# Gated linear attention into a GELU feed-forward on one core: the first three units recast as six chunks with head halves on the partition halves

## The chip, the cores and the metric

The kernel runs on one core of one Trainium2 chip. The metric is device time in microseconds of one execution, given as the median of several runs. The engines are TensorE (PE in the views, with PEld for its weight loads), VectorE (DVE), ScalarE (ACT), GpSimd (POOL) and SyncE (SP, which here only issues transfers). Each takes its own instructions in the order in which the program lists them.

## The reference

Attention with a per-channel decay (a recurrence over 768 positions, 4 batches, 8 heads of 48 channels), and on its output a feed-forward network with exact GELU:

```python
f = 1.0 / (1.0 + np.exp(-f_logit))
for t in range(S):
    state = f[:, :, t, :, None] * state + np.einsum('bhd,bhe->bhde', k[:, :, t], v[:, :, t])
    y[:, :, t] = np.einsum('bhd,bhde->bhe', q[:, :, t], state)
x = y.transpose(0, 2, 1, 3).reshape(B * S, H * D)      # 3072 x 384
h = x @ w_in                                           # 384 x 2048
g = 0.5 * h * (1.0 + erf(h / sqrt(2)))
out = g @ w_out                                        # 2048 x 384
```

## The kernel before

The 3072 rows are 24 chunks of 128 positions, six to a batch. Two chunks make a unit; there are 12 units. Inside a chunk the recurrence is written as masked matrix products; between chunks a state of 48 x 48 per head is carried.

For each unit the steps are these. `decays` takes `fl` (the logits) through exp and ln on ACT (L494, L497), sums the logarithms along the positions on PE with a triangular matrix (L521, or L526/L527 with `trip` for paired units; L515 and L523 give the chunk's total), and makes `rg` and `gt`, the exponentials of minus and plus the sums (L543, L549). DVE multiplies k and q by them (L576) into `sc`; `vb` is v in bf16 (L583). `turn` transposes `sc` on PE (L611) and copies the result to `kq` (L617), or from unit 4 on uses a DMA transpose (L599). PE makes the scores (L722, paired L784), DVE masks them (L631), PE multiplies them by v (L758, paired L826) and adds the part from the carried state (L699, paired L705). The state product is L745 (paired L806); `carry` updates the state: `rr` on DVE (L655), `tn` on POOL (L657), and two copies into the diagonal blocks of `sb` (L662), whose other blocks stay zero. `outputs` copies y to `yb` (L675), transposes it (L691) and copies it to `xT` (L694).

Units 0 to 4 are paired (`PAIRS`): partition p of a tile holds positions 2p and 2p+1 of a stretch of 256, so that a load moves runs of 384 bytes rather than 192. The 64 upper partitions are then the second chunk of the unit. The output rows are put back in order by the gelu, which writes `gT` with a permuted pattern.

`ffn_group` takes one unit's 256 rows: eight F1 steps (L875, six matmuls each) fill a PSUM bank, gelu (L885) writes `gT`, and per chunk four F2 steps (L896, four matmuls each, one for each piece `wout0` to `wout3`) sum into another bank. The result goes through `osb` (L901) to DRAM (L906). Four PSUM banks (`s_fh`) are shared by F1, F2 and, for early units, sums and transposes; the other four by the rest of the attention.

Transfers are in a list, `LOADS`. SP issues the inputs (L449 paired, L457 for the rest), POOL the weights (L461 `win`, in pieces of 1024, 512 and 512 columns; L464 `wout`). Before the first piece of `win` stand f, k, v, q of units 0 and 1; unit 2's come after it, then the rest of `win` and `wout`, then unit 3. A transfer that follows one from the other queue waits for an earlier one there to land (`gate`).

The order on each engine comes from a planner, `Plan.run`, which places the operations one after another by priority. Here the priorities are formulas plus random offsets from `SEEDS`. Where the plan leaves PE idle in the first 30 us, matmuls on a zero tile `junk` (L947) are put in. ACT needs a table load (L953) at each change between exp/ln and gelu.

Of the kernel before, what the change touches and what calls it, by code (L numbers as in the profile page):

```python
# [2 lines left out]

# [9 lines left out]
ALU = mybir.AluOpType  # L13

LAT = {"PE": 0.25, "ACT": 0.16, "DVE": 0.14, "POOL": 0.12, "DMA": 1.0}
TABLE = 1.28

# [2 lines left out]
SHARED = 0.5  # L22

TURN = 0.1

SPREAD, SEED = (1.0, 97)

SEEDS = [1643, 41, 3215, 1275, 2533, 2502, 823, 887, 1264, 763, 2447, 3095]

NUDGE = {}  # L30
XA = 0.0

EAGER = 0.0

# [50 lines left out]
class Plan:  # L85

    def __init__(self):
        self.ops, self.w, self.r = [], {}, {}  # L90

# [24 lines left out]
    def run(self):  # L116
        free = dict.fromkeys(list(LAT), 0.7)
        free["DMA"] = 1.8
        rng = random.Random(SEED)
        own = [random.Random(x) for x in SEEDS]  # L120
        for o in self.ops:
            if o.prio > -5:
                k = min(max(int(o.prio % 1000) // 20, 0), len(SEEDS) - 1)
                o.prio += rng.uniform(-SPREAD, SPREAD)
                if SEEDS[k]:
                    w = (0.5, 1.0, 3.0, 8.0)[SEEDS[k] % 4]
                    o.prio += own[k].uniform(-w, w)
            o.prio += NUDGE.get(o.name, 0.0) + (XA if o.table == "exp" and o.prio > 40 else 0.0)
        act, switched, mode = None, 0.0, 0
        port = {"DVE": (0.0, 0.0), "POOL": (0.0, 0.0)}  # L130
        for o in self.ops:
            o.outs = []
        for o in self.ops:
            o.left = len(o.deps)
            for d in o.deps:
                d.outs.append(o)
        ready = [o for o in self.ops if not o.left]
        placed = []
        while ready:
            best = None  # L140
            for o in ready:
                t = free[o.eng]
                for d in o.deps:
                    v = d.end if d.eng == o.eng and (o.eng != "DMA" or d is o.chain) else d.vis + o.lag
                    t = v if v > t else t
                ok, taken = True, {}
                for b in o.bufs:
                    if b.slot is None:
                        v, k = b.slots.free(), taken.get(id(b.slots), 0)
                        if len(v) <= k:  # L150
                            ok = False
                            break
                        t = max(t, v[k][0])
                        taken[id(b.slots)] = k + 1
                if not ok:
                    continue
                x = t
                if o.table and act and o.table != act:
                    x = max(t, min(t + 2 * TABLE, max([d.vis for d in o.deps] + [switched]) + PATIENCE))
                pr = o.prio + (HOLD if o.held and act == "gelu" else 0.0)  # L160
                key = (int((x - (EAGER if o.eng == "PE" and o.prio < 900 else 0.0)) * 20 + 0.999), pr, o.seq)
                if best is None or key < best[0]:
                    best = (key, t, o)
            if best is None:
                raise RuntimeError("no operation can be placed: %s" % [o.name for o in ready[:20]])
            _, t, o = best
            d = o.dur
            if o.eng == "PE" and o.mode != mode:
                mode = o.mode
                d += TURN  # L170
            if o.port:
                other = port["POOL" if o.eng == "DVE" else "DVE"]
                d += SHARED * max(0.0, min(other[1], t + d) - max(other[0], t))
            if o.table and o.table != act:
                act, switched = o.table, t
                d += TABLE
            o.start, o.end = t, t + d
            o.vis = o.end + o.lat
            free[o.eng] = o.end
            for b in o.bufs:  # L180
                if b.slot is None:
                    b.slot = b.slots.free()[0][1]
                    b.slots.who[b.slot] = b
                b.slots.memo = None
            ready.remove(o)
            placed.append(o)
            if o.port:
                port[o.eng] = (t, o.end)
            for n in o.outs:
                n.left -= 1  # L190
                if not n.left:
                    ready.append(n)
        if len(placed) != len(self.ops):
            raise RuntimeError("operations that wait for each other")
        placed.sort(key=lambda o: (o.start, o.seq))
        self.placed = placed
        return placed

SIZES = [2, 2, 2, 2, 2, 2, 2, 2, 2, 2, 2, 2]
PAIRS = [0, 1, 2, 3, 4]
WIN = [1024, 512, 512]
EG = [0, 1]
ET = [0, 1]
EX = [0]
EA = [0]
SPLIT = []  # L220
HVC = [1]
HKQ = [0, 2, 6]
HYB = [1, 5]
HX = [4]
GKP, GQP = ([2], [3])
GAM = []
ODVE = [0, 1, 2, 4, 6, 7, 8, 9, 10, 11, 12, 13, 14, 16, 17, 18, 19, 20, 21, 22, 23]
XDMA = [5, 6, 7, 8, 9, 10, 11]
KDMA = [4, 5, 6, 7, 8, 9, 10, 11]
AJ = [2, 3, 4, 5, 6, 7, 8, 10, 11]  # L230
NGT = 4
GLD = []
G1D = [2, 3, 4]
YJ = [2, 3, 4]
ROWS = [16, 17, 18, 19]
AMX = []
WARM = 30.0
LOADS = ['f0', 'k0', 'v0', 'q0', 'f1', 'v1', 'k1', 'q1', 'i0', 'k2', 'f2', 'v2', 'q2', 'i1', 'i2', 'i3', 'o0', 'o1', 'o3', 'o2', 'f3', 'k3', 'q3', 'u4', 'v3']
LOADS += [f"u{n}" for n in range(12) if f"u{n}" not in LOADS and f"c{2 * n}" not in LOADS and f"f{n}" not in LOADS]


@with_exitstack
def kernel(
# [59 lines left out]
    s_sb = slots(3, [C, P2, 2 * D], BF16, "sb")  # L303
    s_yb = slots(3, [C, 2, HD], BF16, "yb")
    s_os = slots(4, [C, d_model], F32, "osb")
    s_xT = {s: slots({1: 4, 2: 4}.get(s, 2), [C, s, KO, C], BF16, f"xT{s}") for s in set(SIZES)}
    s_gT = {s: slots({1: 4, 2: NGT}.get(s, 2), [C, FO, s * C], BF16, f"gT{s}") for s in set(SIZES)}
    banks = [pp.tile([C, 512], F32, name=f"ps{i}") for i in range(8)]
    nf, na, _ = BANKS
    s_fh, s_m = Slots(nf, banks[:nf]), Slots(8 - nf - na, banks[nf + na:])  # L310
# [9 lines left out]
    P.add("POOL", 0.5, lambda: make_identity(nc, ident), wr=["ident"], prio=-90)  # L320
    P.add("POOL", 0.5, lambda: tri(mask, 1.0), wr=["mask"], prio=-80)
    P.add("POOL", 0.1, lambda: nc.gpsimd.memset(negcol, -1.0), wr=["negcol"], prio=-79)

    def pair_sums():
# [32 lines left out]
    z_gl = [f"glz{i}" for i in range(6)]  # L359
    z_lf = [f"lfz{i}" for i in range(3)]  # L360
    z_sc = [f"scz{i}" for i in range(NQ)]
    z_sb = [f"sbz{i}" for i in range(3)]

    G = [dict(xT=s_xT[SIZES[g]].new(), gT=s_gT[SIZES[g]].new()) for g in range(NG)]
# [2 lines left out]
        for j in range(SIZES[g]):  # L367
            grp[first[g] + j] = (g, j)
    X = [{} for _ in range(NCH)]
    U = [dict(fl=s_fl.new(), lf=s_lf.new(), pair=u in PAIRS, **{nm: s_in[nm].new() for nm in s_in}) for u in range(NU)]  # L370

    def half(u, b, j):

# [2 lines left out]
        return b.t().rearrange("p (j h d) -> p j h d", j=2, d=D)[:, j]  # L376

    order, pools = [], []  # L380

    def load(eng, issue, wr, bufs, dur, name):
        i = len(order)
        gate = None
        if i and order[i - 1][0] != eng:
            back = 4 if eng == "pool" else 2
            for j in range(i - back, -1, -1):
                if order[j][0] != eng:
                    gate = order[j][1]
                    break  # L390

        def fn(o):
            ins = issue()
# [30 lines left out]
    def srcp(a, u):  # L424
        b, c = divmod(2 * u, nC)
        return a[b, :, c * C:(c + 2) * C, :].rearrange("h (p j) d -> p h (j d)", j=2)

    win_src = moe_w_in.rearrange("(kk p) f -> p kk f", p=C)
    wo_src = moe_w_out.rearrange("(r p j) m -> r p j m", r=4, j=4)
    for what in LOADS:  # L430
        m = int(what[1:])
        if what[0] in "ucfkqv":
            js = (0, 1)
            if what[0] == "c":
                js, m = (m % 2,), m // 2
# [31 lines left out]
    def decays(u):  # L467
# [37 lines left out]
        for j, n in enumerate(ns):  # L505
# [68 lines left out]
            for w, nm, a, b, off in ((0, "kp", "kt", rg, 0), (1, "qp", "qt", gt, 1)):  # L574
# [8 lines left out]
            P.add("ACT" if hv else "POOL", 0.40 if hv else 0.47, lambda y=y, j=j, hv=hv: (nc.scalar.copy if hv else nc.gpsimd.tensor_copy)(  # L583
                y["vb"].t().rearrange("p (h d) -> p h d", h=H), half(u, x["vt"], j)),
                rd=[("vt", n)], wr=[("vb", n)], bufs=[y["vb"], x["vt"]], prio=pr, name=f"VC{n}")

    St = {}

# [177 lines left out]
    def attn_pair(u):  # L766
# [86 lines left out]
        for cc, n in enumerate(ns):  # L853
            outputs(n, yps[cc])

    def ffn_group(g):
        s, t = SIZES[g], G[g]
        xT, gT = t["xT"], t["gT"]
# [9 lines left out]
        for u in range(FO // pk):  # L868
# [10 lines left out]
                  wr=[("h", g, u)], bufs=[xT, hps, gT], prio=pr, opens=hps, name=f"F1.{g}.{u}")  # L879
            def gelu(u=u, hps=hps):  # L880
                to, fr = gT.t()[:, u * pk:(u + 1) * pk, :].rearrange("p a b -> p (a b)"), hps.t()
                if U[ns[0] // 2]["pair"]:
                    to = to.rearrange("p (n t j) -> p n j t", j=2, t=64)
                    fr = fr.rearrange("p (n j t) -> p n j t", j=2, t=64)
                nc.scalar.activation(to, fr, AF.Gelu)  # L885
            P.add("ACT", 0.60 if U[ns[0] // 2]["pair"] else 0.50, gelu, rd=[("h", g, u)], wr=[("gT", g, u)], bufs=[hps, gT], table="gelu", prio=pr - 1000,
                  name=f"GE{g}.{u}")
        for s_ in range(s):
            n = first[g] + s_
# [3 lines left out]
            for r in range(4):  # L893
                def f2(s_=s_, r=r, op=op):
# [6 lines left out]
            P.add("DVE" if od else "ACT", 0.475 if od else 0.40, lambda op=op, osb=osb, od=od: copier(not od)(osb.t(), op.t()[:, 0:d_model]),  # L901
                  rd=[("o", n)], wr=[("os", n)], bufs=[op, osb], prio=pr - 1000, name=f"O{n}")
            def store(n=n, osb=osb):
                w = C // 2 if n in ROWS else C
                for r in range(0, C, w):
                    nc.sync.dma_start(out=out[n * C + r:n * C + r + w, :], in_=osb.t()[r:r + w, :])  # L906
# [18 lines left out]
                name=f"st{n}")  # L925

    g = 0
    for u in range(NU):
        decays(u)
        (attn_pair if U[u]["pair"] else attn_nat)(u)  # L930
        while g < NG and first[g] + SIZES[g] <= 2 * u + 2:
            ffn_group(g)
            g += 1
# [53 lines left out]
```

## Time and profile before

| | |
|---|---|
| median of 3 runs | 182.42 us (182.16 to 182.50) |
| span of the profiled execution | 181.1 us |
| granted PE clock | 1.000 |
| PE, DVE, ACT, POOL busy | 171.7, 96.3, 125.2, 53.6 us |
| DMA | 32.61 MB, mean 180 GB/s |
| gelus on ACT (L885) | 96, 57.5 us, 671 ns each |
| table loads on ACT (L318, L953) | 16, 1283 ns each |
| first F1 matmul, last matmul's end | 20.67, 178.1 us |

The span runs from the first to the last instruction of the execution that was profiled; that execution has no separate time of its own in the results, so the 1.3 us between the span and the median of the runs are what lies around it. Matmuls overlap, so the mean duration of one (273 ns for L875) is not the distance between two (109 ns); for costs the distance is used. Bytes are counted as they arrive: weights are read as float32 and arrive as bf16.

### The profile page before, as it was taken

What the parts mean: (1) busy time and instruction counts of PE and PEld (TensorE: products, weight loads), DVE (VectorE), ACT (ScalarE), POOL (GpSimd) and SP (SyncE); (2) the same over time, 40 slices, a digit from 0 to 9 for tenths busy, and PEclk for the clock granted to TensorE, in tenths of its full rate; (3) what the DMA queues carried; (4) which work ended last, traced back from release to release, by engine and by line L of the source; (5) the groups of instructions that cost most, each with busy time, mean ns of one, the idle gap of its engine ahead of it and who ended that gap; (6) DMA issues with size and microseconds to landing.
All of it is one profiled execution on the core that took longest, in us unless ns stands there. A gap on an engine that the chain in (4) does not pass through costs nothing.

```text
span 181.1 us, 4916 instructions
## 1 busy us (share of the span) xinstructions
PE 171.7 (95%) x1990; PEld 132.3 (73%) x1990; DVE 96.3 (53%) x194; ACT 125.2 (69%) x212; POOL 53.6 (30%) x116
## 2 busy tenths in 40 slices
PE   7788889999999999988999999999999999999993
PEld 2356669966787688785779689976697986886972
DVE  5289750058898564244896692527691625362110
ACT  2775198963899189999967759777585578560720
POOL 7657870003043641140176113112435110300000
PEclk9999999999999999999999999999999999999999
DMA  6999999949997898999999999999999872814102
GB/s 148 261 261 226 268 170 203 200 115 267 278 266 142 186 197 170 249 227 171 216 179 213 215 175 207 195 187 189 185 245 181 181 162 47 166 37 91 43 0 87
DMA packets 106998, 32.61 MB, mean 180 GB/s; under 512 B 102113, under 2 KB 106081, under 8 KB 106977
## 3 DMA queue, kind: packets, MB, share of 16 engines
q1 hardware_dynamic: 105056, 29.07, 79.7%
q0 software_dynamic: 1776, 3.15, 9.8%
q8 instruction: 15, 0.25, 0.6%
q10 hardware_dynamic: 144, 0.10, 0.2%
q14 instruction: 7, 0.05, 0.1%
HBM read 25.17 MB, written 4.72 MB: 165 GB/s over the span
## 4 chain that ended last, share of the span: by engine, by line
PE 64%; ACT 15%; DMA 15%; SPq 3%; issue 1%; DVE 0%; DVEq 0%
PE ps L875 26%; PE ps L896 25%; ACT gT L885 7%; DMA fl<-in_f_logit_dram 7%; DMA win<-in_moe_w_in_dram 5%; ACT L953 4%; SPq L449 3%; DMA kq<-sc 2%; PE ps L722 2%; PE ps L758 2%; PE ps L917 1%; ACT gt L549 1%; PE ps L521 1%; PE ps L699 1%; PE ps L745 1%
## 5 line engine op out<-in xcount | busy, mean ns | idle before, releaser
L885 ACT ACTIVATE gT<-ps 128x512 bf16<-128x512 f32 x96 | 57.5, 671 | 24.6 <-PE ps L875 23.0
L875 PE MATMUL ps<-xT,win 128*128 128x256 bf16 x576 | 68.7, 273 | 1.3 <-ACT gT L885 0.9
L896 PE MATMUL ps<-wout,gT 128*128 128x384 bf16 x368 | 66.0, 326 | 0.0
L875 PEld LDWEIGHTS <-win 128*128 128x128 bf16 x576 | 61.6, 114 | 3.9 <-issue 1.2
L896 PEld LDWEIGHTS <-gT 128*128 128x128 bf16 x368 | 34.2, 98 | 19.5
L583 POOL CAST vb<-vt 128x384 bf16<-128x384 f32 x22 | 12.6, 584 | 52.5 <-DMA vt<-in_v_dram 52.4
L631 DVE TENSOR_TENSOR am<-ps,mask 128x512 bf16<-128x512 f32 x28 | 17.6, 684 | 15.1 <-PE ps L722 15.1
L901 DVE COPY osb<-ps 128x384 f32<-128x384 f32 x20 | 11.1, 556 | 25.9 <-PE ps L896 18.2
L657 POOL TENSOR_TENSOR tn<-rr,gl 128x384 f32<-128x384 f32 x16 | 14.0, 872 | 35.2 <-DVE rr L655 34.6
L576 DVE TENSOR_TENSOR sc<-qt,gt 128x384 bf16<-128x384 f32 x23 | 14.0, 616 | 13.7 <-ACT gt L549 13.7
L576 DVE TENSOR_TENSOR sc<-kt,rg 128x384 bf16<-128x384 f32 x23 | 13.5, 597 | 11.3 <-ACT rg L543 11.3
L953 ACT ACT_TABLE_LOAD x15 | 19.2, 1283 | 0.3
L662 POOL CAST sb<-tn 48x192 bf16<-48x192 f32 x40 | 14.8, 371 | 11.6 <-DVE tn L651 6.6
L494 ACT ACTIVATE fl<-fl 128x768 f32<-128x768 f32 x12 | 10.1, 842 | 10.5 <-DMA fl<-in_f_logit_dram 10.5
L675 DVE CAST yb<-ps 128x384 bf16<-128x384 f32 x22 | 11.9, 555 | 7.4 <-PE ps L758 3.7
L631 DVE TENSOR_TENSOR am<-ps,maskp 128x512 bf16<-128x512 f32 x20 | 12.5, 684 | 2.2 <-PE ps L784 1.4
L543 ACT ACTIVATE rg<-ps 128x384 f32<-128x384 f32 x21 | 10.3, 503 | 4.4 <-PE ps L523 2.8
L549 ACT ACTIVATE gt<-ps 128x384 f32<-128x384 f32 x21 | 10.2, 503 | 3.9 <-PE ps L523 3.3
L947 PE MATMUL ps<-junk 128*128 128x512 bf16 (+3 forms) x36 | 10.4, 423 | 2.1 <-POOL junk L939 1.3
L655 DVE TENSOR_TENSOR rr<-ps,tn 128x384 f32<-128x384 f32 x16 | 8.9, 553 | 3.5 <-POOL tn L657 1.8
L497 ACT ACTIVATE lf<-fl 128x768 bf16<-128x768 f32 x12 | 10.1, 843 | 0.4
L947 PEld LDWEIGHTS <-junk 128*128 128x128 bf16 x36 | 3.6, 111 | 6.2 <-issue 3.5
(74 smaller groups left out, 130.4 us busy)
## 6 DMA issues: line engine op xcount, KB each, us to landing
out_dram<-osb SPq DMA_DIRECT2D x19, 192.0 KB, 3.1
fl<-in_f_logit_dram SPq DMA_DIRECT2D x14, 192.0 KB, 3.8
kt<-in_k_dram SPq DMA_DIRECT2D x14, 192.0 KB, 3.8
qt<-in_q_dram SPq DMA_DIRECT2D x14, 192.0 KB, 3.7
vt<-in_v_dram SPq DMA_DIRECT2D x14, 192.0 KB, 3.9
fl<-in_f_logit_dram SPq DMA_DIRECT2D x5, 384.0 KB, 6.2
kt<-in_k_dram SPq DMA_DIRECT2D x5, 384.0 KB, 6.2
vt<-in_v_dram SPq DMA_DIRECT2D x5, 384.0 KB, 5.7
```

What stands on the lines that cost most here:

```text
L549: P.add("ACT", 0.40, lambda g=gps[j], gtv=gtv: nc.scalar.activation(gtv(), g.t()[:, 0:HD].rearrange("q (p h d) -> q p h d", h=2, d=D), AF. ...
L576: P.add("POOL" if pl else "DVE", 0.80 if pl else 0.475, lambda a=a, y=y, j=j, w=w, pl=pl, b=(gtv if w else rg): (nc.gpsimd if pl else nc.v ...
L583: P.add("ACT" if hv else "POOL", 0.40 if hv else 0.47, lambda y=y, j=j, hv=hv: (nc.scalar.copy if hv else nc.gpsimd.tensor_copy)(y["vb"].t ...
L631: P.add("POOL" if pl else "DVE", 1.15 if pl else 0.61, lambda hh=hh, pl=pl: (nc.gpsimd if pl else nc.vector).tensor_tensor(ams[hh].t(), ap ...
L657: P.add("POOL", 0.83, lambda: nc.gpsimd.tensor_tensor(tn.t(), rr.t(), glb(), ALU.mult), rd=[("rr", n), ("gl", n)], wr=[("tn", n)], bufs=[r ...
L662: P.add("POOL", 0.36, lambda hh=hh: nc.gpsimd.tensor_copy(sb.t()[64 * hh:64 * hh + D, :, D * hh:D * hh + D], tn.t()[64 * hh:64 * hh + D, : ...
L675: P.add("ACT" if help_ else "DVE", 0.40 if help_ else 0.475, lambda: copier(help_)(yb.t()[:, i, :], yp.t()[:, 0:HD]), rd=[("yp", n)], wr=[ ...
L875: nc.tensor.matmul(hps.t()[:, i * tok:(i + 1) * tok].rearrange("a (s t) -> a s t", s=s), col(fo)[:, kk, :], xT.t()[:, :, kk, :], start=(kk ...
L885: nc.scalar.activation(to, fr, AF.Gelu)
L896: nc.tensor.matmul(op.t()[:, 0:d_model], gT.t()[:, fo, s_ * C:(s_ + 1) * C], wout[fo // 4][:, fo % 4, :], start=(fo == 0), stop=(fo == FO ...
L947: nc.tensor.matmul(o.opens.t()[:, 0:w], junk[:, 0:C], junk[:, 0:w], start=True, stop=True, skip_group_check=True)
L953: nc.scalar.preload_act_table_set({"exp": "natural_log_exp_and_others", "gelu": "gelu_and_others"}[o.table])
```

## The change

Units 0, 1 and 2 leave `PAIRS` (now 3 and 4) and become `HALVES`. Each chunk is loaded, and worked on, by itself. A chunk's tile has 64 partitions for heads 0 to 3 and 64 for heads 4 to 7 (`s`), and partition p of a half holds positions 2p and 2p+1 (`j`). Each tensor of a chunk comes in two transfers of 96 KB. `sc`, `kq` and the scores keep their tile sizes. `vx` holds v with one head half per partition half and zeros elsewhere, so that one matmul serves both head halves. The state product gives the 48 x 48 blocks without the zero blocks, so the tiles of the state (`rr`, `tn`) have half the width; `sb` is written from `rr` directly.

The list of loads puts five of the six chunks ahead of the first weight piece, and the sixth between the first and the second. `win` comes in four pieces of 512 columns. The random offsets are gone; a list `PRIO` of 978 numbers gives each operation's priority. For units 0 to 4 the gelu writes in plain order, and the store puts the rows in order, in two transfers for each chunk. Several lists that say which engine makes a copy are changed, and the joined form of scores and outputs (`AJ`, `YJ`) and the sums by subtraction (`G1D`) are used in other units.

In the new program's order of instructions, the matmul counts of the feed-forward part are the same (576, 368 and 32); table loads number 20 with the first, junk matmuls 24 after 36.

```diff
-PAIRS = [0, 1, 2, 3, 4]
-WIN = [1024, 512, 512]
-EG = [0, 1]
-ET = [0, 1]
+PAIRS = [3, 4]
+HALVES = [0, 1, 2]
+RST = [0, 1, 2, 3, 4, 5, 6]
+VA = [(0, 0), (4, 0)]
+WIN = [512, 512, 512, 512]
+EG = [0, 1, 2]
+ET = [0, 1, 2]
...
-AJ = [2, 3, 4, 5, 6, 7, 8, 10, 11]
+AJ = [3, 4, 5, 6, 7, 8, 9, 10, 11]
-G1D = [2, 3, 4]
-YJ = [2, 3, 4]
+G1D = [3, 4, 5, 6]
+YJ = [4, 5, 6]
+AHEAD = 4.4
-LOADS = ['f0', 'k0', 'v0', 'q0', 'f1', 'v1', 'k1', 'q1', 'i0', 'k2', 'f2', 'v2', 'q2', 'i1', 'i2', 'i3', 'o0', 'o1', 'o3', 'o2', 'f3', 'k3', 'q3', 'u4', 'v3']
+LOADS = ['F0', 'K0', 'Q0', 'V0', 'F1', 'K1', 'Q1', 'F2', 'V1', 'K2', 'Q2', 'V2', 'F3', 'K3', 'Q3', 'F4', 'V3', 'K4', 'Q4', 'V4', 'i0', 'F5', 'K5', 'Q5', 'V5', 'i1', 'i2', 'i3', 'o0', 'o1', 'o2', 'o3', 'q3', 'f3', 'k3', 'v3', 'f4', 'k4', 'v4', 'q4', 'u5', 'u6', 'u7', 'u8', 'u9', 'u10', 'u11']
...
+        if PRIO:
+            for o, p in zip(self.ops, PRIO):
+                o.prio = p / 20
...
-            back = 4 if eng == "pool" else 2
-            for j in range(i - back, -1, -1):
-                if order[j][0] != eng:
+            ahead = 0.0
+            for j in range(i - 1, -1, -1):
+                if order[j][0] != eng and ahead >= (AHEAD if eng == "pool" else 1.4):
                     gate = order[j][1]
                     break
+                ahead += order[j][1].dur
...
+    def srcx(a, n, s):
+        b, c = divmod(n, nC)
+        return a[b, 4 * s:4 * s + 4, c * C:(c + 1) * C, :].rearrange("h (p j) d -> p h (j d)", j=2)
...
+                for s in range(2):
+                    load("sp", lambda b=U[m // 2][nm], a=a, m=m, s=s: nc.sync.dma_start(
+                        out=part(b, m % 2)[64 * s:64 * s + 64].rearrange("p (h x) -> p h x", h=4), in_=srcx(a, m, s)),
+                        [(nm, m, s)], [U[m // 2][nm]], LX, f"{nm}{m}")
...
+            def cum(lv=lv, g=g):
+                gv = g.t()[:, 0:HD].rearrange("p (j h d) -> p j h d", j=2, d=D)
+                for jo in range(2):
+                    for i in range(2):
+                        nc.tensor.matmul(gv[:, jo], trip[:, 0 if i <= jo else 1, :], lv()[:, i, :, 0:D],
+                                         start=(jo == 0 and i == 0), stop=(i == 1), skip_group_check=True)
...
+            old, rr = St["t"], s_rr.new()
+            P.add("DVE", 0.29, lambda: nc.vector.tensor_tensor(small(rr), spf(), small(old), ALU.add),
...
+            for hh, r in enumerate(rows):
+                P.add("POOL", 0.40, lambda hh=hh, r=r: nc.gpsimd.tensor_tensor(sb.t()[r, :, D * hh:D * hh + D], small(rr)[r], glb(r), ALU.mult),
...
+            P.add("POOL", 0.45, lambda: nc.gpsimd.tensor_tensor(small(tn), small(rr), glb(), ALU.mult),
...
+                                nc.tensor.matmul(aps[hh].t()[t, at:at + C], kq.t()[r, 0, 2 * jk + pp, c, t], kq.t()[r, 1, 2 * pp + s, c, :],
+                                                 start=True, stop=True)
...
+                                nc.tensor.matmul(sp.t()[64 * hh:64 * hh + 64, 0:HD // 2].rearrange("a (s p e) -> a s p e", s=2, p=2)[:, :, pp],
+                                                 sc.t()[:, 0, 4 * j + 2 * pp + hh, :], vx.t()[:, j, :, e:e + D],
+                                                 start=(j == 0 and pp == 0), stop=(j == 1), skip_group_check=True)
...
+                            nc.tensor.matmul(yp.t()[:, 0:HD].rearrange("a (s e) -> a s e", s=2)[:, :, e:e + D], ams[hh].t()[:, 2 * pp + jk, :],
+                                             vx.t()[:, jk, :, e:e + D], start=(osb is None and hh == 0 and pp == 0 and jk == 0),
+                                             stop=(hh == 1 and pp == 1 and jk == 1), skip_group_check=True)
...
-                if U[ns[0] // 2]["pair"]:
+                if perm(ns[0]) and ns[0] // 2 not in RST:
                     to = to.rearrange("p (n t j) -> p n j t", j=2, t=64)
...
+                if perm(n) and n // 2 in RST:
+                    for j in range(2):
+                        nc.sync.dma_start(out=out[n * C:(n + 1) * C, :].rearrange("(r j) m -> j r m", j=2)[j], in_=osb.t()[64 * j:64 * j + 64, :])
+                    return
...
-        decays(u)
-        (attn_pair if U[u]["pair"] else attn_nat)(u)
+        (decays_hs if U[u]["hs"] else decays)(u)
+        (attn_hs if U[u]["hs"] else attn_pair if U[u]["pair"] else attn_nat)(u)
```

In this form `[("sp", n)]` and the other dependencies are written by chunk, so that a chunk's steps do not wait for the unit's other chunk.

## The prediction

> **What bounds the kernel now.** I read the summary of engines first, then the shares of the chain that ended last, then that chain in order of time, then stretches.
>
> ```profile
> PE 171.7 (95%) x1990; PEld 132.3 (73%) x1990; DVE 96.3 (53%) x194; ACT 125.2 (69%) x212; POOL 53.6 (30%) x116
> PE 64%; ACT 15%; DMA 15%; SPq 3%; issue 1%; DVE 0%; DVEq 0%
> ```
>
> TensorE (PE) is the bound over the whole, but 18% of the chain are transfers and their issue. The chain in time shows where:
>
> ```profile
> 4.38 6.17 DMA fl<-in_f_logit_dram
> 10.55 0.30 issue
> 10.84 9.78 DMA win<-in_moe_w_in_dram
> ...
> 20.67 2.16 PE ps L875 x18
> ...
> 25.61 0.73 ACT gT L885
> 26.34 0.04 issue
> 26.38 1.13 PE ps L947 x5
> 27.52 1.32 PE ps L875 x12
> 28.86 7.43 ACT gT L885 x12
> ```
>
> Columns: start, length, what. The feed-forward (FFN) part cannot start before the first weight transfer lands at 20.63 us. From 25.61 to 27.52 PE waits for the first gelu and fills in with five junk matmuls (L947). The reason stands in ScalarE's (ACT's) timeline:
>
> ```profile
> 22.56 0.84 ACT L494 ACTIVATE fl<-fl 128x768 f32<-128x768 f32 x1 [3.89 <-DMA fl<-in_f_logit_dram]
> 23.43 0.85 ACT L497 ACTIVATE lf<-fl 128x768 bf16<-128x768 f32 x1
> 24.30 1.28 ACT L953 ACT_TABLE_LOAD   x1
> 25.59 2.53 ACT L885 ACTIVATE gT<-ps 128x512 bf16<-128x512 f32 x4
> ```
>
> Unit 2's decays land behind the weights, ACT waits 3.89 us for them, does exp and ln, and only then loads the gelu table.
>
> How much is lost in all? Durations are spacings in the chain and the timeline: 6 matmuls of L875 in 0.655 us (0.109 each), 4 of L896 in 0.65 (0.1625), 32 of L917 in 2.65 (0.083). That makes 576 x 0.109 + 368 x 0.1625 + 2.6 = 125.2 us for the FFN. The attention matmuls counted the same way (transposes 0.055, L784 0.018, L826 0.016, L705 0.029, L806 0.028, L699 and L745 0.043, L722 0.034, L758 0.025, the 128x384 sums 0.16, the one- and two-column sums 0.02) give 31.4. Useful work is 156.6 us and PE ends at 178.1. By counts in the stretches up to 20.6 us, 6.7 us of it are done before the first F1 matmul; so after it 157.4 us pass for 149.9 us of work: **7.5 us are lost after 20.67**, about 1.8 of them in the hole above, the others in waits of under half a microsecond (0.44 at 55, 0.45 at 79, 0.37 at 84 us) and at changes of matmul shape.
>
> **What the Trainium skill says.** "DMA: Bandwidth & Descriptors", section Rules for kernel authors, says of two transfers to disjoint partition halves "Don't bother — they serialize", and advises one 128-partition transfer. Its section on the anatomy of a DMA puts a fixed cost of some 2.0 us on each, which more of them in flight hide. The trace has no half-partition load; its 96 KB stores land in 2.2 us, which agrees with the fixed cost. "ScalarE: Activation LUTs", section What ACT_TABLE_LOAD costs, gives 1283 ns for the load plus about 1380 ns of drain per switch: the trace has the 1283 ns, but gelu starts 0.01 us after the load (24.30 + 1.28, then 25.59), so I price a switch at 1.28. "TensorEngine Tiling (Array Packing)", section Key Properties, says that a change of tiling mode drains TensorE; the trace shows nothing I can separate.
>
> **The change part by part.**
>
> *Loads.* Twelve 384 KB loads become 48 of 96 KB; the bytes and the 384-byte runs stay. In the rates of the first 20.67 us, HWDGE loads run at 260 to 263 GB/s, so 98 KB need 0.375 us. SP's shortest issues are 0.37 to 0.39 us each, so issue and transfer just about balance, and I keep the rate. Up to 20.67 us the DMA view of that stretch counts 3.95 MB for the HWDGE queue and 0.79 for the weight queue; weights arrive as bf16, so 1.57 MB were read and 5.5 MB in all. Now 20 chunk loads (3.93 MB) and a first weight piece half as wide (0.79) precede F1: 4.7 MB at the same 5.5/18.9 = 0.29 MB per us end at 1.8 + 16.2 = 18.0 us, or 20.7 if all of chunk 5 shares the engines equally. In the new PE order the first F1 also stands behind the first scores of chunk 4, whose inputs land near 17 and take some 3 us (fl at 4.4, scores possible about 10 for unit 0, less for half the elements). I take **20.0: -0.7 us** (bounds -2, +1).
>
> *PE work moved ahead.* By the order of instructions, the cumulative sums, transposes and scores of chunks 0 to 4, four state products and three outputs come before the first F1: 5 x 0.42 + 40 x 0.055 + 80 x 0.018 + 32 x 0.028 + 24 x 0.043 + 8 x 0.043 + 9 x 0.056 = 8.6 us against 6.7: **-1.9**. It is all under the transfers.
>
> *The hole at 25.6.* First gelu after the change: chunk 5's fl lands at about 20, then exp and ln (half of 0.84 each), sums, two exps, transposes' copy and the 1.28 us table: 24 to 25.5, about as now. But PE then still has 3.9 us of attention (sums and transposes of chunk 5, outputs 3 and 4) to put beside four F1 groups (2.6 us, as many as PSUM holds): 20.0 + 6.5 = 26.5. The hole closes: **-1.7**. Late next are weights: columns come in four pieces, and PE asks for piece 1 at about 24 and piece 3 at 28. From 20.67 to about 37 us 2.36 MB of bf16, so 4.7 read, and 1.0 of loads arrived, 0.35 MB per us, 2.25 us a piece: about 23, 25 and 27.5. **+0.6** for two near misses (0 to +3).
>
> *PE work added.* Units 0 to 2: cumulative matmuls 24 of 192 columns (half of 0.16) for 10 of 384: +0.3; new outputs 48 of 96 columns with 128 rows (as L745, 0.043) for 96 x 0.016: +0.5; state products 40 x 0.03 for 40 x 0.028; old-state outputs 20 x 0.043 for 40 x 0.029: -0.3. Scores and transposes keep count and shape. **+0.6** (to +1.2; to +2.5 if 192 columns cost as much as 384).
>
> *ACT.* Gelus of groups 0 to 4 lose their permuted write: 7.43/12 = 0.62 against 6.16/11 = 0.56 for the plain ones, 40 x 0.06 = -2.4. Table loads go from 16 to 20: +5.1. ACT is 69% busy and PE waits for its gelus 0.9 us in two places, so I count nothing; uncovered it costs up to 2.7, and a well placed switch may equally save the 0.9.
>
> *DVE, POOL.* State tiles halve (R 0.55, T 0.87), the two copies into sb read rr directly rather than tn, so one POOL step leaves the chain of states: some 0.8 us a chunk, beside transfers that need 3.1 us a chunk, so nothing. Five added zeroings (0.2 each) lie ahead of the first DVE work at 7.75. DVE has for six chunks 10 x 0.5 + 8 x 0.4 + 12 x 0.62 + 5 x 0.4 + 6 x 0.4 = 20 us to do between 6 and about 28: nearly full, but the last chunks are wanted only by F1 groups from about 30 on. POOL's weight issues (0.8 each) stand behind chunk 1's state; late there means late weights, counted in the range.
>
> *Stores.* Ten chunks are stored in 20 transfers: ten more SP issues at 0.58 (median of L906), between 43 and 75 us, past which unit 5's loads and the first DMA transposes are moved. Nothing, as PE there has F2 work of two groups; uncovered up to +2. Loads of unit 3 wait, as now, for the third wout piece (SP idle 16.8 us for it), and q3 now precedes f3: 1.5 us on a path with slack.
>
> *The rest.* A new written-out list of priorities reorders all engines after 45 us. Of the 7.5 us lost, 5.7 lie in such small waits; the list may take or add: -3 to +3, I take 0.
>
> Sum: -0.7 - 1.9 - 1.7 + 0.6 + 0.6 = **-3.1 us**: span 181.1 to 178.0. The median of the runs, 182.42, has 1.3 us around that span, so 179.3.
>
> **Rivals.**
> 1. *Slower: half loads don't keep the rate.* Each half waits for the eighth before it, so 0.79 MB are in flight; if a half takes 0.5 us rather than 0.385, the 40 ahead of F1 end 4.6 us later and nothing covers that: -3.1 + 4.6, 183.9 us. It decides from 0.385 + 3.1/40 = 0.46 us a half. For it: the skill's rule, and issue times at the edge. Against: 0.79 MB cover 3 us at 262 GB/s and small transfers land in 2.2.
> 2. *More gain.* The new order also halves the 5.7 us of small waits: 176.4. For it: the six chunks are done before FFN crowds PSUM and ACT. Against: from 100 us on PE is never idle in the stretches.
> 3. *No gain.* Attention is early, but F1 then starves on pieces of win and wout, the same 4.7 MB as before behind it: +3.1, 182.4. This is also the case that "ahead of the weights" does nothing, as F1 needs both.
>
> **How the numbers follow.** Likeliest case 0.43, rival 2 0.21, rival 3 0.16, rival 1 0.20. What a measurement here can tell from no change is 0.2%, 0.36 us. Faster 0.43 + 0.21 + 0.06 = 0.70; same 0.05; slower 0.25. The likeliest case alone spans 177.3 to 181.3; with rival 2 at its far end (-7) and rival 1 up to 0.5 us a half the range is 175.3 to 184.0.
>
> **What would show it.** Right: first F1 at 19 to 21 us, no junk matmul between 24 and 30, V5's landing by 23, F1 waits for win under 1 us. Wrong: halves spaced over 0.46 us, or a first gelu after 28; then rival 1. Long PE waits on win or wout: rival 3. A lead at 45 us that is gone at 100 would put the fault in "the rest".

## The result, and the profile after

The change makes the kernel slower: 204.13 us median of four runs (203.45 to 205.3), against 182.46 for the kernel before in the same comparison; the ratio is 1.120 [1.116, 1.124]. The profiled execution has a span of 203.3 us, 22.2 more than before, at a mean granted PE clock of 0.958. The prediction was 179.3 with a range up to 184.0. Comparisons leave out one run of a later kernel that was slow as a whole (189.88 us, over 1.5% above that kernel's fastest).

The kernel before was profiled in one of its longer executions: the 38 other executions for which a span is known have a median of 180.2 us, and each took 1.8 to 2.1 us more than its span. So the 1.3 us given above is not what lies around a span; the profiled execution, at 181.1, was 0.9 us longer than the usual one, and differences under 1 us against its trace mean little.

The summary of engines, three rows of the span in 40 slices of 5.1 us, and the shares of the chain that ended last, of the changed kernel:

```profile
PE 178.6 (88%) x1922; PEld 138.0 (68%) x1922; DVE 96.1 (47%) x198; ACT 131.4 (65%) x231; POOL 56.8 (28%) x123
...
PE   6773829899999999699879998599999999999993
...
PEclk9996666999999999999999999969999999999999
DMA  3665797999899975989989999999799993723112
...
PE 53%; DMA 21%; SPq 12%; DVE 8%; issue 2%; ACT 2%; POOL 1%; DVEq 0%; ACTq 0%; POOLq 0%
```

PE's busy time grew by 7 us, with fewer matmuls, while its share of the chain fell from 64% to 53%. What rose are SP's queue (3% to 12%), transfers (15% to 21%) and DVE. The DMA row is the odd one: in the first 20 us, where everything waits for loads, the DMA engines are only about 60% busy. The granted clock is about 0.6 from 15 to 35 us, in slices in which PE is busy between 0.2 and 0.9 of the time.

The chain in time shows what the slices can't (start, length, what):

```profile
18.56 0.61 SPq L475
19.18 0.04 issue
19.22 0.61 SPq L475
...
22.52 5.76 DMA vt<-in_v_dram
...
32.89 6.90 DMA vt<-in_v_dram
```

This is a ladder: SP issues one half load (L475), 0.61 us, and 0.04 later the next. In the timeline of SP it begins with the second tensor, long before anything could be full:

```profile
0.74 1.44 SPq L475 DMA_DIRECT2D fl<-in_f_logit_dram  x2
2.22 1.28 SPq L475 DMA_DIRECT2D kt<-in_k_dram  x2
...
26.48 1.27 SPq L475 DMA_DIRECT2D vt<-in_v_dram  x2
```

So a half costs 0.66 us of SP from the start; only one of the 40 on the way takes clearly longer (1.13). The last line is chunk 4's v; 40 halves are issued at 27.75 us. The DMA view of the first 20 us gives the rate that comes of it:

```profile
DMA packets 7074, 2.58 MB, mean 129 GB/s; under 512 B 7073, under 2 KB 7073, under 8 KB 7073
```

98 KB per 0.66 us is 149 GB/s, where the kernel before moved 260 (from 2 to 12 us; 227 over the same first 20).

The start of the feed-forward part, in the timelines of PE and ACT:

```profile
35.45 0.82 PE L1116 MATMUL ps<-xT,win 128*128 128x256 bf16 x6
```

```profile
39.35 1.28 ACT L1198 ACT_TABLE_LOAD   x1
40.65 1.80 ACT L1126 ACTIVATE gT<-ps 128x512 bf16<-128x512 f32 x3
```

The first F1 matmul comes at 35.45 rather than 20.67: +14.8. That is not all. From there to PE's end 164.7 us pass, 157.4 before, though by the prediction's count 1.9 us of work had been moved ahead. A second loss of some 7 us lies after the start. PE's waits hint at it, with two names that the kernel before had small or not at all:

```profile
PE ps L659 <- ACT lf L651: 3.8, 3, 1.6
PE ps L732 <- DVE sc L675: 3.4, 1, 3.4
...
PE ps L1116 <- DMA xT<-yb: 2.9, 2, 2.1
...
PE ps L960 <- DMA kq<-sc: 1.2, 2, 0.9
```

Columns: us in all, times, longest. The first two are waits of the start, on engines that themselves wait for loads. The last two are on DMA transposes, which SP issues, in the same queue as the stores:

```profile
74.20 3.79 SPq L1147 DMA_DIRECT2D out_dram<-osb  x6
78.09 1.81 SPq L503 DMA_DIRECT2D qt<-in_q_dram  x1
```

Six half stores (L1147) hold SP for 3.79 us before the next q is issued.

### The profile page after: what moved, and what is told of

Same layout as the page of the kernel before. It is cut to its first block, busy times and chain, and to the rows that moved or that the text cites. A ratio compares the mean times of both kernels' runs of the same rounds, so it can differ in the third digit from the quotient of the medians.

```text
span 203.3 us, 4876 instructions
## 1 busy us (share of the span) xinstructions
PE 178.6 (88%) x1922; PEld 138.0 (68%) x1922; DVE 96.1 (47%) x198; ACT 131.4 (65%) x231; POOL 56.8 (28%) x123
## 4 chain that ended last, share of the span: by engine, by line
PE 53%; DMA 21%; SPq 12%; DVE 8%; issue 2%; ACT 2%; POOL 1%; DVEq 0%; ACTq 0%; POOLq 0%
PE ps L1116 24%; PE ps L1137 21%; SPq L475 12%; DMA vt<-in_v_dram 6%; DMA xT<-yb 5%; DMA fl<-in_f_logit_dram 3%; DMA wout<-in_moe_w_out_dram 3%; DVE sc L622 3%; DVE am L869 2%; DMA qt<-in_q_dram 2%; PE ps L960 2%; DMA kq<-sc 2%; PE ps L1162 1%; PE ps L996 1%; DVE rr L893 1%
## 5 line engine op out<-in xcount | busy, mean ns | idle before, releaser
L1126 ACT ACTIVATE gT<-ps 128x512 bf16<-128x512 f32 x96 | 55.0, 599 | 28.4 <-PE ps L1116 25.9
L1137 PEld LDWEIGHTS <-gT 128*128 128x128 bf16 x368 | 34.9, 99 | 22.5 <-issue 1.7
L900 POOL CAST sb<-tn 48x192 bf16<-48x192 f32 x30 | 10.7, 355 | 14.8 <-DVE tn L889 9.8
L622 DVE TENSOR_TENSOR sc<-kt,rg 128x384 bf16<-128x384 f32 x18 | 10.5, 594 | 8.2 <-ACT rg L589 8.2
L622 DVE TENSOR_TENSOR sc<-qt,gt 128x384 bf16<-128x384 f32 x18 | 11.0, 625 | 5.2 <-DMA qt<-in_q_dram 2.7
L895 POOL TENSOR_TENSOR tn<-rr,gl 128x384 f32<-128x384 f32 x12 | 10.1, 840 | 11.6 <-DVE rr L893 5.9
L540 ACT ACTIVATE fl<-fl 128x768 f32<-128x768 f32 x9 | 7.6, 844 | 4.3 <-DMA fl<-in_f_logit_dram 4.2
L732 PE MATMUL ps<-ident,sc 128*128 128x128 bf16 x48 | 6.2, 278 | 4.1 <-DVE sc L675 3.4
L682 POOL CAST vx<-vt 64x384 bf16<-64x384 f32 x10 | 5.2, 526 | 14.1 <-DMA vt<-in_v_dram 14.0
L767 DVE TENSOR_TENSOR am<-ps,maskp 128x512 bf16<-128x512 f32 x12 | 7.7, 683 | 3.0 <-PE ps L762 3.0
L732 PEld LDWEIGHTS <-sc 128*128 128x128 bf16 x48 | 4.2, 124 | 6.5 <-DVE sc L675 5.3
```

The source lines that it names most:

```text
L622: P.add("POOL" if pl else "DVE", 0.80 if pl else 0.475, lambda a=a, y=y, j=j, w=w, pl=pl, b=(gtv if w else rg): (nc.gpsimd if pl else nc.v ...
L732: nc.tensor.transpose(tpv(w)[:, b * C:(b + 1) * C], sc.t()[:, w, 2 * b:2 * b + 2, :], ident)
L900: P.add("POOL", 0.36, lambda hh=hh: nc.gpsimd.tensor_copy(sb.t()[64 * hh:64 * hh + D, :, D * hh:D * hh + D], tn.t()[64 * hh:64 * hh + D, : ...
L1137: nc.tensor.matmul(op.t()[:, 0:d_model], gT.t()[:, fo, s_ * C:(s_ + 1) * C], wout[fo // 4][:, fo % 4, :], start=(fo == 0), stop=(fo == FO ...
```

## The experiments

The theory after this reading: each half load costs SP 0.66 us, and that alone makes the first 15 us of the loss; the half stores make the rest. Rivals: the new form itself (its PE order, POOL's smaller pieces, ACT's added table loads) is slow, and late loads only show it. In the code below `...` marks lines left out.

### The loads alone, in the kernel before

Units 0 to 2 of the kernel before, with everything else left, load each tensor in pieces. `CUTS` gives the pieces as slices of partitions and of heads:

```diff
-                    load("sp", lambda x=x, nm=nm, a=a, m=m: nc.sync.dma_start(
-                        out=x[nm].t().rearrange("p (h x) -> p h x", h=H), in_=srcp(a, m)),
...
+                        for ps, hs in (CUTS if m < 3 else [(slice(0, C), slice(0, H))]):
+                            ins = nc.sync.dma_start(out=x[nm].t().rearrange("p (h x) -> p h x", h=H)[ps, hs], in_=srcp(a, m)[ps, hs])
...
```

First, quarters of 64 partitions and four heads, the shape of the change:

```diff
+CUTS = [(slice(p, p + 64), slice(h, h + 4)) for p in (0, 64) for h in (0, 4)]
```

> The kernel before with only this: each of the twelve loads of units 0 to 2 goes as four transfers of 64 partitions x 4 heads x 96 (96 KB), the shape of the changed kernel; all else stays. Theory 'issue on SP': each such transfer takes SP 0.66 us as in the changed kernel, so 48 of them need 32 us where twelve needed 18.5; fl of unit 2 lands near 29 rather than 22.6, first gelu near 32, 188 to 191 us. Rival 'order': the loss of the changed kernel comes from its list of priorities and the plan; then splitting alone costs under 1 us, 182.2 to 183.5.

Measured: 195.39 us (195.06 to 195.75), ratio 1.072 [1.069, 1.075]. First F1 at 33.7, 156.4 us from there to PE's end, as good as before. That is 4 us more than the theory's 188 to 191, and far from the rival's 182.2 to 183.5. SP's timeline has the same price, 0.65 us each:

```profile
3.53 2.60 SPq L452 DMA_DIRECT2D kt<-in_k_dram  x4
```

The shape of the loads alone costs 13 us, all of it ahead of the first F1 (33.7 against 20.67). What about the shape does it? Two kernels with two pieces of 192 KB separate the number of partitions from the number of transfers.

```diff
+CUTS = [(slice(p, p + 64), slice(0, 8)) for p in (0, 64)]
```

> The kernel before with the loads of units 0 to 2 in two transfers of 64 partitions x 8 heads x 96 (192 KB, 512 runs of 384 bytes each). If an issue costs 0.62 us whatever its size, 24 of them take 16 us, less than the data need, and the time stays at 182 to 184. If the cost is per run (0.62 for 256), they take 1.25 us each, 30 us in all, and the time is 188 to 191 as with quarters.

```diff
+CUTS = [(slice(0, 128), slice(h, h + 4)) for h in (0, 4)]
```

> The same with two transfers of 128 partitions x 4 heads x 96 (192 KB, 512 runs). Per-transfer cost: 182 to 184. Per-run cost: 188 to 191. If the 64 partitions are what makes an issue slow, this one is fast (issues of about 0.4 us) and the 64 x 8 one is slow.

Measured, one run each: 188.69 us with 64 partitions, 182.77 with 128. Same bytes, same number of transfers, same 384-byte runs. A line of SP's timeline and the DMA view from 2 to 12 us, first of the kernel with 64 partitions, then of that with 128:

```profile
3.59 1.31 SPq L452 DMA_DIRECT2D vt<-in_v_dram  x2
...
DMA packets 5446, 2.03 MB, mean 203 GB/s; under 512 B 5446, under 2 KB 5446, under 8 KB 5446
```

```profile
2.89 1.06 SPq L452 DMA_DIRECT2D vt<-in_v_dram  x2
...
DMA packets 7077, 2.64 MB, mean 264 GB/s; under 512 B 7077, under 2 KB 7077, under 8 KB 7077
```

Two things come with 64 partitions. An issue takes 0.65 us, whether it moves 96 or 192 KB, against 0.53 with 128; and even at 192 KB, where the issue no longer limits (192 KB per 0.65 us would be 300 GB/s), the transfers run at 203 rather than 264 GB/s. So the issue has neither one price per transfer nor one per run; it is the third case that was expected, the 64 partitions. Why 64 partitions are slow, in issue or in transfer, these traces do not show. Splitting a tensor by heads costs 0.5 us here, in a single run: next to nothing.

### A second queue for the halves

In the changed kernel, ACT issues the second half of each tensor:

```diff
-                    load("sp", lambda b=U[m // 2][nm], a=a, m=m, s=s: nc.sync.dma_start(
+                    load("sp", lambda b=U[m // 2][nm], a=a, m=m, s=s: (nc.scalar if s else nc.sync).dma_start(
```

> The changed kernel with the second half of each pair (heads 4 to 7) issued by ACT rather than SP; order and bytes stay. Theory 'issue on SP': SP has 24 issues of 0.66 us, 16 us, the last v of chunk 5 lands at 22 to 27 us rather than 37 (ACT pays 24 x 0.6 us of its own time, so it may lag), first F1 at 22 to 28 rather than 35.5, and the time is 187 to 196. Rival 'order': first F1 may come earlier, but the time stays over 200.

Measured: 201.87 us (200.44 to 202.64), ratio 1.109 [1.105, 1.113]. The first F1 comes at 30.5, 5 us earlier, and 165.1 us pass after it. From 2 to 20 us two queues reach 203 GB/s. That is the figure of the kernel with halves of 64 partitions above, but not shown to be the same limit: there the DMA engines are busy throughout, here they have gaps (82% in the queues' shares). The start gains no more than 5 us because ACT's issues are drawn out to 30 us, in line with its own exponentials and logarithms. An early and the last issue in ACT's timeline:

```profile
10.97 0.60 ACTq L475 DMA_DIRECT2D vt<-in_v_dram  x1
...
30.39 0.69 ACTq L475 DMA_DIRECT2D vt<-in_v_dram  x1
```

The medians are 2.3 us apart; the two profiled executions, the slowest of the changed kernel's four and the fastest of these, are 4.6 apart in span. The time is the one that the rival expected, over 200 us, and this run alone does not refute it; the next ones do.

### The changed kernel with one full-width load for two halves

```diff
-                        out=part(b, m % 2)[64 * s:64 * s + 64].rearrange("p (h x) -> p h x", h=4), in_=srcx(a, m, s)),
...
+                        if not s:
+                            whole[nm, m] = nc.sync.dma_start(
+                                out=part(b, m % 2).rearrange("p (h x) -> p h x", h=4), in_=srcp(a, m // 2)[:, 4 * (m % 2):4 * (m % 2) + 4])
...
```

> The changed kernel, order and all else kept, but each chunk's tensor comes in one transfer of 128 partitions x 4 heads x 96 (192 KB, the shape that took 0.53 us to issue in the run with head halves) in place of two of 64 partitions. It leaves out the right placing of the data: heads and positions land in the wrong rows, so its output is not the reference's, but bytes, runs and instructions are those of the change. Theory 'loads are all of it': first F1 at 19 to 22 us, and with the waits after F1 gone too, 178 to 181 us. Rival 'a second loss after F1': in the changed kernel and in the run with two queues PE needs 165 us from the first F1 to its end where before needs 157; if that is the new order or the stores, first F1 comes at 19 to 22 but the time is 186 to 190.

Measured: 187.96 us (187.09 to 188.72), ratio 1.034 [1.030, 1.037]. First F1 at 22.5, and 159.6 us from there to PE's end instead of 164.7. The half loads account for 16.2 of the 21.7 us: 12.9 ahead of the first F1, the rest after it. The time is in the range of the rival, a second loss after F1. With 128 partitions the mean clock is 0.998: the low clock went with the starved start. That the clock follows from the starving, and what it adds of its own, was not tried by itself. Among the four runs of the changed kernel the one with the highest mean clock (0.958, the others 0.932 or 0.933) was the slowest.

### The stores alone, in the kernel before

Units 0 to 4 of the kernel before get the plain gelu and the two half stores of 64 rows:

```diff
-                if U[ns[0] // 2]["pair"]:
-                    to = to.rearrange("p (n t j) -> p n j t", j=2, t=64)
-                    fr = fr.rearrange("p (n j t) -> p n j t", j=2, t=64)
...
+                if U[n // 2]["pair"]:
+                    for j in range(2):
+                        nc.sync.dma_start(out=out[n * C:(n + 1) * C, :].rearrange("(r j) m -> j r m", j=2)[j], in_=osb.t()[64 * j:64 * j + 64, :])
+                    return
```

> The kernel before with one part of the change alone: for units 0 to 4 gelu writes in plain order and the store puts the rows in order in two transfers of 64 rows. ACT saves about 40 x 0.06 = 2.4 us, off the path for the most part, SP issues ten transfers more. If stores cost nothing: 181.5 to 182.5. If the stores (and their 64-partition shape) hold up the loads behind them on SP: 183 to 187.

Measured: 185.97 us (185.82 to 186.46, without the run of 189.88), ratio 1.022 [1.019, 1.024]: slower by 3.9 us, although the permuted gelus are gone. A pair of half stores keeps SP 1.1 to 2.0 us, where one store kept it 0.58 in the median; all ten pairs together keep it 13.4 us, the ten single stores 9.0. The transposes behind come later and PE waits for them; two of PE's waits in this kernel:

```profile
PE ps L875 <- DMA xT<-yb: 2.0, 2, 1.5
PE ps L722 <- DMA kq<-sc: 1.6, 2, 0.9
```

The kernel before has no wait of the first kind, and 0.4 us of the second. The added 3.2 us are about what is lost after the first F1: 160.4 us to PE's end, against 157.4. In SP's timeline of this kernel the transposes of `kq` that the kernel before issues at 92.17 stand behind a pair of stores:

```profile
92.91 1.22 SPq L903 DMA_DIRECT2D out_dram<-osb  x2
94.24 3.10 SPq L599 DMA_TRANSPOSE kq<-sc  x2
```

### The changed kernel with single stores

```diff
-RST = [0, 1, 2, 3, 4, 5, 6]
+RST = []
```

The planned duration of the gelu is kept, so that the order stays.

> The changed kernel with that part undone: gelu writes permuted, each chunk's result is stored in one transfer of 128 rows; the order on PE, ACT, DVE and POOL stays. The half loads stay, so first F1 stays at about 35. If the store split is what costs the 8 us after F1: 196 to 199. If it is the order or the late start: 203 to 206 (ACT pays 2.4 us more).

Measured: 198.53 us (196.95 to 198.82), ratio 1.088 [1.084, 1.093]. First F1 at 36.3 and 156.9 us to PE's end: the second loss is gone with the half stores. It is not the stores alone, though. With full-width loads and half stores 159.6 us passed, so half stores cost some 3 us there, and 6 to 8 where the loads are late as well. This kernel has the starved start too, at a still lower clock (0.5 from 10 to 35 us, mean 0.93), so with single stores that start does no harm to what follows it. Its own start is 0.9 us later than the changed kernel's, with the same issues of SP; the lower clock may be the reason.

### Both repairs together

> Both: loads of 128 partitions (data in the wrong rows, as in e6) and gelu ordering with single stores. If loads and stores are the two causes, 178 to 181 and below e6 by several us; if the stores don't matter, within 1 us of e6.

Measured: 184.92 us (183.65 to 186.2), ratio 1.015 [1.010, 1.021]; first F1 at 23.04, 156.3 us to PE's end. Loads and stores explain 19.2 of the 21.7 us, less than the 16.2 and 5.6 of the single repairs together: going back to single stores gains 5.6 us with half loads, 3.0 with full-width ones. Why late loads make the half stores dearer was not tried. What is left is a kernel slower than before by 1.5%, 2.8 us, above the 178 to 181 that were expected; 2.4 of the 2.8 are the later first F1. The chain in time of this kernel runs through POOL up to its second F1 step (24.74; the first, at 23.04, is not on it):

```profile
17.58 1.30 POOL vx L686 x2
18.95 1.00 POOL sc L679
19.94 0.78 POOL sb L716
20.78 0.73 POOL sb L716
21.50 2.30 POOL win L511 x3
```

In this kernel a cast into `vx` is one of ten of 64 partitions, 0.62 us each in the mean, where one of 128 partitions in the kernel before took 0.58. So half the partitions save nothing, and two casts stand where there was one. That suggested POOL as a third cause.

### POOL's work taken out

The casts on POOL copy one of four heads; in the second kernel the multiplications into `sb` are cut in the same way too:

```diff
-                    vx.t()[64 * s:64 * s + 64, :, s, :].rearrange("p j (h d) -> p j h d", d=D), jh(part(x["vt"], j)[64 * s:64 * s + 64])),
+                    vx.t()[64 * s:64 * s + 64, :, s, :].rearrange("p j (h d) -> p j h d", d=D)[:, :, 0:4 if va else 1], jh(part(x["vt"], j)[64 * s:64 * s + 64])[:, :, 0:4 if va else 1]),
```

> The kernel with whole-chunk loads and plain store order (184.9 us, first F1 23.0), in which the casts of v into vx that POOL makes for the six chunks (L686, ten of 64x384, 6.1 us in all) copy only the first of four heads, so that three quarters of v's columns are left out there; order, planned durations and all waits stay. Theory (POOL is the third loss: its queue of casts, multiplications and weight issues holds back the states and the first weight piece between 17 and 27 us): some 3 to 4 us of POOL work go, first F1 at 20.5 to 22, time 182 to 183.5. Rival (the order on PE or ACT's table loads hold the start, POOL is beside it): first F1 stays at 22.5 to 23.2, time 184.4 to 185.2.

```diff
-                P.add("POOL", 0.40, lambda hh=hh, r=r: nc.gpsimd.tensor_tensor(sb.t()[r, :, D * hh:D * hh + D], small(rr)[r], glb(r), ALU.mult),
+                P.add("POOL", 0.40, lambda hh=hh, r=r: nc.gpsimd.tensor_tensor(sb.t()[r, 0:1, D * hh:D * hh + D], small(rr)[r, 0:1], glb(r)[:, 0:1], ALU.mult),
```

> As the run before, and POOL's multiplications into sb (L716, eight of 48x192, 5.0 us) make one of four head pairs only. Theory: another 2 to 3 us of POOL's work go, partly behind other limits by then: first F1 at 20 to 21.5, time 181 to 183. Rival: no change against the kernel without it, 184.4 to 185.2.

Measured: 184.82 us (184.17 to 184.99) and 184.37 (183.16 to 185.12), ratios 1.013 [1.010, 1.015] and 1.010 [1.007, 1.013]. First F1 at 23.40 and 22.25. The theory missed both times; they are the rival's. POOL was on the chain, but with its casts shortened the chain goes over another path with the same end. With the second edit the first F1 comes 0.8 us earlier than without either, and the intervals of the time overlap. The chain of the second shows what takes POOL's place:

```profile
13.73 5.10 DMA vt<-in_v_dram
18.88 0.39 issue
19.27 0.49 ACT rg L670
...
21.07 0.42 PE ps L766 x16
```

Even with most of this work of POOL gone the transfer issued at 13.73, chunk 4's v, lands near 18.9, and 3.4 us of attention steps follow before the first F1 at 22.25. By the medians this work costs 0.1 us (casts) to 0.6 us (both); the spread of the runs does not separate that from nothing.

### ACT's table loads taken out

The gelu is replaced by an exponential, which needs no other table, in the kernel before and in the kernel with both repairs:

```diff
-                nc.scalar.activation(to, fr, AF.Gelu)
+                nc.scalar.activation(to, fr, AF.Exp, scale=0.01)
...
-            if o.dur:
+            if o.dur and o.table == "none":
                 nc.scalar.preload_act_table_set({
```

> The kernel before, in which the gelu is replaced by an exponential of a hundredth of its input, which needs no other table: so the gelu itself and all 15 table loads at 1.28 us between are left out, and the order on every engine, the other durations and the waits stay. With the next run it asks whether what is left of the loss in the kernel with fast loads and plain store order (184.9 us, where the sum asked for some 3 us less than before after the first F1 matmul and 0.9 were found) is ACT with its four more table loads. Either theory expects the first gelu 1.3 us earlier and the hole at 25.6 shorter by as much: 179.5 to 181.2.

> The kernel with whole-chunk loads (v and the others lie in the wrong rows) and plain store order (184.9 us), with the same replacement: no gelu and none of the 19 table loads between. Theory (ACT's added table loads are not covered): it gains 2 us or more beyond what the kernel before gains by the same edit, thus 180 to 181.5 and within 1 us of the run before. Rival (the loss is the late start, 2.4 us at the first F1, and PE's own order; ACT is covered): it gains as much as the kernel before or less, and stays 2 to 3 us above the run before: 182.5 to 184.

Measured: 180.71 us (180.48 to 181.38), ratio 0.992 [0.989, 0.994]; and 184.18 (183.58 to 184.82), ratio 1.011 [1.007, 1.015]. The kernel before gains 1.3 us by losing its 15 table loads, the repaired one 0.7 (against its 184.92 above) by losing 19. The two stay 3.5 us apart, a little more than the rival's 2 to 3 and far from the theory's 1: the four added switches, 5.1 us of ACT, are covered. No version that computes the reference and beats the kernel before came out of these runs.

## Why the prediction was wrong

**Loads: the step that failed.** It put a half at 0.375 us, "issue and transfer just about balance", and kept the rate. Measured: 0.66 us of issue. The error was to read 0.37 to 0.39 us, the shortest issues of 128-partition transfers, as the price of an issue whatever its shape. The kernel before had transfers of 64 partitions and 96 KB to read instead: its stores of chunks 16 to 19 go out in halves of 64 rows, which took SP 1.20 us for two, 1.11 for two and 2.47 for four, thus 0.55 to 0.62 each, about as long as a store of 128 rows in the same kernel (0.57 at 91.50 us).

Forty halves at 0.66 end at 27.75 us, where the kernel with both repairs has issued the same chunks by 15.31. In both, the first F1 follows 7.7 us after that (35.45 and 23.04): ACT waits for chunk 4's v to land, until 30.77 and 18.68, and 4.7 and 4.4 us of steps follow. So the first F1 is 12.4 us later for this reason, and removing it gains 16.2 us in the time, as the half stores cost less then.

Rival 1 named the place and the observation that would show it (halves spaced over 0.46 us), and got a fifth of the chance; the range went only as far as 0.5 us a half. At the rival's own slope, 40 x (0.66 - 0.385), it gives 190.3, closer than anything else in the prediction. The mechanism inside it was another, though: SP does not wait for the eighth half before, as the ladder starts at 2 us with DMA engines 60% busy; the issue itself is long.

"DMA: Bandwidth & Descriptors", section Rules for kernel authors, of the Trainium skill, quoted in the prediction, said "Don't bother — they serialize" of transfers to disjoint partition halves. The runs agree with the advice and go further: with 192 KB halves by partition 203 GB/s and 188.69 us, with halves by head 264 GB/s and 182.77. The prediction cited the rule and then overruled it with an issue time that it had for the other form only.

**Stores: the second step that failed.** "Nothing, uncovered up to +2." Measured: 3.9 us in the kernel before, 5.6 in the changed kernel, 3.0 in it with full-width loads. The step looked at what PE does while the rows go out. It named the transposes moved behind the stores, and did not price what happens when these come late: PE waits for them.

**First F1 at 20.0.** With loads at full rate it is 23.04, and 22.25 without most of POOL's work. The step had the inputs of chunk 4 at 17, and "some 3 us" after; the last of them landed at 18.7 to 18.9, and 4.4 us follow, 3.4 without most of POOL's work. Bounds of -2 and +1 were too narrow by 1 to 2 us.

**After the first F1.** With both repairs 156.3 us pass, against 157.4: a gain of 1.1 where the terms -1.9, -1.7 and +0.6 gave 3.0. Even the 1.1 are not sure, as the profiled execution of the kernel before was 0.9 us longer than its usual one; the kernel with halves by head, which differs from it in the loads alone, takes 156.2. For the same reason up to 0.9 of the 7.5 us that the prediction counted as lost may belong to that one execution. The hole at 25.6 shrank, but did not close: PE is idle 0.67 us at 26.3 and fills 0.2 with junk. From 40 us to the end of the middle stretches at 160, PE is idle 2.3 us, against 1.4 in the kernel before and 0.9 in that with halves by head. These two take back 1.8 to 2.3 us of the gain that was expected. Which part of the written-out order makes the later idling is open.

**ACT, PE's added work, DVE.** That ACT's added switches are covered held. POOL, costed at nothing, was off by 0.1 to 0.6 us by the medians, not clear of the spread. PE's added work and DVE's were not tried alone; in the repaired kernel they are part of what is named above.

**Rivals 2 and 3.** Neither was tested as such, since F1 started too late. In the repaired kernel no wait on `win` or `wout` appears among PE's waits, so rival 3's starving of weights is not seen; nor is rival 2's larger gain.

## What to carry to other kernels

Before a load or store is cut in two, take its issue time from a row of the same form: one with half the partitions is not half of one with all of them. If a tensor must be cut, cut it along the free axis. And cost an added transfer by what stands behind it in its queue: two half stores for one, ten times, cost 3 to 6 us here, in a kernel with PE busy 95% of the time, because transposes that PE needs are issued by the same engine.

## What the runs showed of the hardware

- A load to 64 partitions took SP 0.61 to 0.66 us to issue, with 96 KB as with 192 KB; one to 128 partitions with 192 KB took about 0.5 us in the first 4 us.
- With 64 partitions and 192 KB from one queue, DMA engines busy throughout, the transfers reached 203 GB/s; with 96 KB from two queues, engines 82% busy, also 203; with 128 partitions 260 to 264.
- A POOL cast of 64x384 took 0.49 us at the least, one of 128x384 0.50.
- With half loads, PE's granted clock fell to 0.6 or 0.7 from 15 to 35 us in the changed kernel and to 0.5 from 10 to 35 us in that with single stores; with full-width loads the mean of the profiled execution was 0.997 or 0.998.
